# Loading four tiles in place of three by halves on both DMA queues, in a channel-attention kernel

## The chip, the cores and the metric

The kernel runs on one core of a Trainium2 chip. The text names the core's engines as the profile does: PE multiplies matrices, DVE and ACT compute on vectors, and SP only issues transfers here. A transfer is issued into a queue, of SP or of ACT, and 16 DMA engines carry out what both queues hold; a transfer has landed when its last byte has arrived and its waiters may go on.

The metric is the device time of one execution in microseconds (us), lower is better. Most executions of the kernel before took between 531.4 and 532.1 us. A few took more, up to 535.26 us, with no change to the kernel; they are in the comparisons.

A ratio is the mean time of one kernel's fast runs over that of the other's fast runs of the same rounds, so it is not quite the ratio of the medians that I quote. A 95% interval is given with it.

## The reference

```python
def reference(x, w1d):               # x: 1 x 384 x 384 x 384, bf16; w1d: one number
    B, H, W, C = x.shape
    g = jnp.einsum("bhwc->bc", x) / (H * W)      # mean of each channel
    s = _sigmoid(g * w1d[0])                     # (cut: with one tap the padding is none)
    return x * s[:, None, None, :]
```

Every byte of `x` (113.25 MB) must be read and every byte of the result written. In principle a result can only be written when the mean is known, that is after all of `x` has been read, and the kernel's buffer holds only six of the 27 tiles into which it cuts `x`. The kernel therefore makes a guess: it computes the gate `s_early` from the first tile alone and multiplies with it while the true mean is still being summed. At the end it compares the guess with the true gate after rounding. Only if they differ would a second pass run; on this input they are equal.

## The kernel before

A tile is 44 rows of 384 channels on each of 128 partitions: 33,792 bytes a partition, 4.33 MB in all. There are 27 tiles, the last two smaller. The buffer is cut into slots of one tile.

```python
EDGE, SLOT, BOTH = 44, 44, 3
...
n_slots = n_arena // SLOT            # six here
...
def load(place, n, r0, queues=("sync",)):      # SP's queue, if nothing else is said
    of = dram(x_rows, r0, n)
    i = 0
    for queue, m in zip(queues, split(n, -(-n // len(queues)))):
        plan.dma(queue, at(place + i, m), of[:, i * C : (i + m) * C],
                 writes=rows(place + i, m))
        i += m
...
def put(place, n, r0, to):           # DVE multiplies, ACT's queue stores
    plan.op("vector", gate(to, place, n, s_early), ...)
    plan.final.append(
        plan.dma("scalar", dram(o_rows, r0, n), at(to, n), reads=rows(to, n)))
...
for k in range(BOTH):                # the first tiles: half on SP, half on ACT
    load(places[k], sizes[k], starts[k], ("sync", "scalar"))
    if k == 0:
        plan.dma("scalar", w_one[0:1, 0:1], w1d.unsqueeze(0), writes=["w_one"])
...                                  # (cut: s_early from tile 0)
for k in range(1, len(sizes)):
    if k >= n_slots:
        j = k - n_slots
        put(places[j], sizes[j], starts[j], places[j])
    if k >= BOTH:
        load(places[k], sizes[k], starts[k])
    add_rows(places[k], sizes[k], 1, k == 1, k == last)    # PE sums the channels
```

Two queues carry the traffic: SP's and ACT's. Loads wait on SP until the store that used their slot has landed. Stores go through ACT when DVE has multiplied.

## Time and profile before

531.52 us, the median of three runs (531.44 to 531.8).

| what | value | where it is read |
|---|---|---|
| span of the profiled run | 530.0 us | head of the page |
| bytes moved, mean rate | 226.64 MB, 428 GB/s | the page's DMA lines |
| PE, DVE busy | 46%, 46% | part 1 |
| load, from issue to landing | 47.4 us | part 6 |
| store, from issue to landing | 53.6 us | part 6 |

These lines are from the page: busy time by engine; the busy share of the 16 DMA engines in 40 slices (9 is 90% or more); packets; and the two large groups of DMA issues with count, KB of each and us to landing.

```profile
PE 246.4 (46%) x865; PEld 96.0 (18%) x865; DVE 241.3 (46%) x45; ACT 2.7 (1%) x4; POOL 0.3 (0%) x5
DMA  8999999999999999999999999999999999999997
DMA packets 8220, 226.64 MB, mean 428 GB/s; under 512 B 914, under 2 KB 914, under 8 KB 914
...
out_dram<-arena ACTq DMA_DIRECT2D x25, 4224.0 KB, 53.6
arena<-in_x_dram SPq DMA_DIRECT2D x22, 4224.0 KB, 47.4
```

The DMA engines are full from the first slice to the last, and nothing else is. The busy shares of PE and DVE say that they have time to spare. That points to the bytes as what sets the time.

Next, stretches of the run in the view of windows. The first number pair is the stretch in us, the last two columns are the busy share of the DMA engines and their rate in GB/s.

```profile
5.00:30.00 25.00, 14.61 (x60) 6.26 (x61) 5.88 (x9) 0.61 (x1) 0.00 (x0) 1.00 1.01 431
30.00:45.00 15.00, 10.93 (x38) 4.15 (x36) 14.70 (x2) 0.00 (x0) 0.00 (x0) 0.77 1.03 422
45.00:60.00 15.00, 9.69 (x38) 3.79 (x36) 10.88 (x2) 0.00 (x0) 0.00 (x0) 0.89 1.00 433
100.00:480.00 380.00, 179.81 (x627) 69.92 (x627) 171.06 (x20) 0.00 (x0) 0.00 (x0) 0.73 1.00 433
525.00:530.00 5.00, 0.00 (x0) 0.00 (x0) 0.00 (x0) 0.00 (x0) 0.00 (x0) 0.50 0.35 151
```

Loads on both queues (5 to 30 us) run at 431 GB/s, loads and stores together at 433.

Last, the timeline. First three groups of matmuls on PE, which start when their tile lands, with the wait in brackets; then SP's issue of a load in the middle of the run, which waits for a store.

```profile
35.83 10.23 PE L186 MATMUL acc<-arena,ones 128*128 128x512 bf16 x33 [4.07 <-DMA arena<-in_x_dram]
49.34 8.63 PE L186 MATMUL acc<-arena,ones 128*128 128x512 bf16 x33 [3.27 <-DMA arena<-in_x_dram]
...
448.62 8.66 PE L186 MATMUL acc<-arena,ones 128*128 128x512 bf16 x33 [9.85 <-DMA arena<-in_x_dram]
...
61.80 0.33 SPq L91 DMA_DIRECT2D arena<-in_x_dram  x1
401.25 0.33 SPq L91 DMA_DIRECT2D arena<-in_x_dram  x1
```

Tile 2 lands at 35.83 us and tile 3 at 49.34 us. SP issues tile 6 at 61.80 us, when the first store has landed.

### The profile page before, as it was taken

To read this page: it belongs to the slowest core of one execution; us is meant where nothing else is said; L and a number is where in the kernel's file an instruction comes from. 1 tells how busy PE (TensorE), PEld (TensorE's weight loads), DVE (VectorE), ACT (ScalarE), POOL (GpSimd) and SP (SyncE) were. 2 spreads that over 40 slices of the span, in tenths; PEclk is the share of its full clock that TensorE was granted. 3 is DMA by queue.
4 is the path that set the end of the run, shared out by engine and by line. 5 is a ranking of instruction groups with operands and counts; after the bars stand their busy time and mean duration, and the time that the engine had idled before them with its cause. 6 is when DMAs were issued, how large, how long until landed. Compare 5 with 4: busy or idle time off the path is not lost.

```text
span 530.0 us, 1952 instructions
## 1 busy us (share of the span) xinstructions
PE 246.4 (46%) x865; PEld 96.0 (18%) x865; DVE 241.3 (46%) x45; ACT 2.7 (1%) x4; POOL 0.3 (0%) x5
## 2 busy tenths in 40 slices
PE   0867362472472562462572562461562562564320
PEld 0322120120120220120220220120220220221100
DVE  0298715516516426516416426516426426416640
ACT  1000000000000000000000000000000000000000
POOL 0000000000000000000000000000000000000000
PEclk9987876876865776876865766876867766867765
DMA  8999999999999999999999999999999999999997
GB/s 356 431 437 407 441 431 434 436 419 449 434 423 439 426 440 434 423 439 444 421 435 428 441 436 421 441 432 431 436 421 446 435 423 439 423 433 435 439 425 320
DMA packets 8220, 226.64 MB, mean 428 GB/s; under 512 B 914, under 2 KB 914, under 8 KB 914
## 3 DMA queue, kind: packets, MB, share of 16 engines
q10 hardware_dynamic: 4322, 119.74, 52.4%
q1 hardware_dynamic: 3888, 106.76, 47.0%
q8 instruction: 7, 0.11, 0.1%
q14 instruction: 3, 0.02, 0.0%
HBM read 113.25 MB, written 113.25 MB: 427 GB/s over the span
## 4 chain that ended last, share of the span: by engine, by line
another core or an unknown queue 66%; DMA 23%; PE 3%; DVE 2%; SPq 1%; issue 0%; ACTq 0%; ACT 0%; DVEq 0%
DMA arena<-in_x_dram 14%; DMA out_dram<-arena 9%; PE acc L186 3%; DVE arena L156 2%; SPq L91 1%; DVE total L208 0%; ACTq L91 0%; ACT s_true L290 0%; DVE total L298 0%; DVE wrong L306 0%; SPq L99 0%; DVE redo L312 0%; DVEq L99 0%
## 5 line engine op out<-in xcount | busy, mean ns | idle before, releaser
L186 PE MATMUL acc<-arena,ones 128*128 128x512 bf16 x864 | 246.3, 456 | 246.6 <-DMA arena<-in_x_dram 246.6
L156 DVE TENSOR_TENSOR arena<-arena,s_early 128x16896 bf16<-128x16896 bf16 (+2 forms) x27 | 234.6, 8691 | 244.8 <-PE acc L186 241.1
L186 PEld LDWEIGHTS acc<-arena,ones 128*128 128x128 bf16 x864 | 95.9, 114 | 396.5 <-DMA arena<-in_x_dram 254.8
L234 PE MATMUL w_all<-w_one,ones 1*128 1x1 bf16 x1 | 0.2, 158 | 14.4 <-DMA w_one<-in_w1d_dram 14.4
L243 DVE TENSOR_SCALAR w_scaled<-w_all 128x1 f32<-128x1 f32 x2 | 0.2, 153 | 13.6 <-PE w_all L234 13.6
L208 DVE TENSOR_TENSOR total<-total,acc 128x128 f32<-128x128 f32 (+2 forms) x11 | 4.5, 408 | 2.1 <-PE acc L186 1.8
L206 DVE COPY total<-acc 128x384 f32<-128x384 f32 x1 | 0.6, 557 | 8.7 <-PE acc L186 8.7
L290 ACT ACTIVATE s_true<-total,w_scaled 128x384 bf16<-128x384 f32 x1 | 0.6, 615 | 483.3 <-DVE total L208 483.3
L234 PEld LDWEIGHTS w_all<-w_one,ones 1*128 1x128 bf16 x1 | 0.1, 101 | 14.3 <-issue 14.3
L228 ACT ACT_TABLE_LOAD x1 | 1.3, 1283 | 3.0 <-issue 3.0
L298 DVE TENSOR_TENSOR total<-s_true,s_early 128x384 f32<-128x384 uint16 x1 | 0.6, 557 | 0.7 <-ACT s_true L290 0.7
L266 ACT ACTIVATE s_early<-total,w_scaled 128x384 bf16<-128x384 f32 x1 | 0.6, 614 | 21.8 <-DVE total L208 21.8
L306 DVE TENSOR_REDUCE wrong<-total 128x1 f32<-128x384 f32 x1 | 0.6, 552 | 0.0
L256 DVE MEMSET ones<- 128x128 bf16 x1 | 0.2, 165 | 0.8 <-PEq L386 0.8
L228 ACT ACTIVATE warm<-warm 128x1 f32<-128x1 f32 x1 | 0.2, 203 | 0.0
L312 DVE CAST redo<-wrong 128x1 int32<-128x1 f32 x1 | 0.2, 153 | 0.0
L386 POOL MEMSET const-bfloat16-1.0<- 128x1 bf16 x1 | 0.1, 101 | 0.0
L386 POOL MEMSET const-uint8-127<- 128x1 uint8 x1 | 0.1, 101 | 0.0
L255 POOL MEMSET warm<- 128x1 f32 x1 | 0.1, 99 | 0.3 <-POOLq L386 0.3
L386 POOL MEMSET const-float32-0.0<- 128x1 f32 x1 | 0.1, 98 | 0.2 <-issue 0.2
L386 POOL MEMSET const-float32-1.0<- 128x1 f32 x1 | 0.1, 98 | 0.0
## 6 DMA issues: line engine op xcount, KB each, us to landing
out_dram<-arena ACTq DMA_DIRECT2D x25, 4224.0 KB, 53.6
arena<-in_x_dram SPq DMA_DIRECT2D x22, 4224.0 KB, 47.4
arena<-in_x_dram ACTq DMA_DIRECT2D x3, 2112.0 KB, 22.6
arena<-in_x_dram SPq DMA_DIRECT2D x3, 2112.0 KB, 22.3
arena<-in_x_dram SPq DMA_DIRECT2D x1, 2688.0 KB, 43.9
out_dram<-arena ACTq DMA_DIRECT2D x1, 2688.0 KB, 26.5
arena<-in_x_dram SPq DMA_DIRECT2D x1, 2304.0 KB, 39.5
out_dram<-arena ACTq DMA_DIRECT2D x1, 2304.0 KB, 23.9
```

The source lines that it names most:

```text
L91: ("op", lambda e: e.dma_start(out, in_), self.pool[i], 16)
L156: return lambda e: e.tensor_tensor(to_v, v, s_b, ALU.mult)
L186: lambda e, i=i, bank=bank: e.matmul(bank[:, :], ones[:], arena[:, start + i * WIDE : start + (i + 1) * WIDE], start=first and i < 3, stop ...
L206: emit = lambda e, part=part, of=of: e.tensor_copy(part, of)
L208: emit = lambda e, part=part, of=of: e.tensor_tensor(part, part, of, ALU.add)
L228: lambda e: e.activation(warm[:, 1:2], warm[:, 0:1], ACT_F.Sigmoid),
L234: lambda e: e.matmul(w_all[:, 0:1], ones[0:1, :], w_one[0:1, 0:1], start=True, stop=True),
L266: lambda e: e.activation(s_early[:], total[:], ACT_F.Sigmoid, scale=w_scaled[:, 0:1]),
L290: lambda e: e.activation(s_true[:], total[:], ACT_F.Sigmoid, scale=w_scaled[:, 1:2]),
L298: lambda e: e.tensor_tensor(total[:], s_true[:].bitcast(U16), s_early[:].bitcast(U16), ALU.not_equal),
L306: lambda e: e.reduce_max(wrong[:], total[:], axis=mybir.AxisListType.X),
L386: nc = _bacc.Bacc("TRN2", target_bir_lowering=False, num_devices=1)
```

## The change

The intent: tile 3, too, comes in on both queues by rows, half of its rows on each.

```diff
-EDGE, SLOT, BOTH = 44, 44, 3
+EDGE, SLOT, BOTH = 44, 44, 4
```

One load of 128 x 16896 elements on SP becomes two of 128 x 8448, one on SP and one on ACT. Bytes, slots, PE and DVE work stay as they are.

## The prediction

> **What bounds the kernel now.** The transfers, all the way through. The page counts 226.64 MB in a span of 530.0 us, a mean of 428 GB/s, with the DMA engines at nine tenths in 38 of 40 slices; PE and DVE are each busy 46%. In five-microsecond windows the rate is 433 GB/s almost everywhere from 5 to 480 us. The exceptions are the start (230 GB/s in the first 5 us), the place where stores join the loads (409 GB/s from 40 to 45 us), and the end (151 GB/s in the last 5 us). The Trainium skill, "DMA: Bandwidth & Descriptors", section "Where 436 GB/s comes from", gives a ceiling of 435 GB/s for the 16 ports; the trace agrees with its 433. An estimate from the trace: 226.6 MB at 433 GB/s is 523 us, so only about 7 us are start, joins and tail.
>
> **What the change does.** Nothing is removed. By the instruction order one load of 128x16896 on the SP queue becomes two of 128x8448, one on each queue; PE, DVE and POOL are unchanged. The cost is one more issue on the ACT queue, 0.36 to 0.42 us in the trace, at about 3 us, when ACT has only its table load to do. Bytes, the five slots and the waits of later tiles stay.
>
> The same page ("Issuing engines are not separate DMA queues") says that both issuers run on the same 16 engines. The trace agrees: loads on both queues (5 to 30 us) run at 429 to 433 GB/s, loads on one and stores on the other at 433. So a second queue brings no rate; it changes the order of bytes.
>
> **The order.** Before, tile 2 lands at 35.8 us and the first store is issued at 35.86 us. By then about 1.4 MB of tile 3 are in (estimate: 33.4 us at 431 GB/s less three tiles of 4.33 MB). Its rest shares the engines with that store and lands at 49.3 us. After: half of tile 3 stands before the first store on the ACT queue, so I expect tile 3 to land at 43 to 46 us, and the first store at 63 to 66 us instead of 61.8. Tile 5 reuses that store's slot, so its load is issued then, about when tile 4 has ended; the SP queue may stand empty for 1 to 4 us. The stores queued on ACT then take the whole rate, so the engines stay busy (stores alone at the tail still run at 415 to 432 GB/s). After one or two tiles the pattern of before returns: a load issued every 19.95 us, landing about 27 us later.
>
> **On the critical path:** the number of bytes, unchanged. Possible gain: the weak stretch from 30 to 42 us (407 GB/s, about 0.7 us lost) may soften. Possible loss, of the same size: where the SP queue runs dry, and in how unevenly the engines finish (the rate falls from 369 to 18 GB/s between 525 and 529 us).
>
> **Time:** 531.3 us, range 529.8 to 533.2. Chances: faster by over 2% 0.01, within 2% 0.97, slower by over 2% 0.02.
>
> **What would show it.** Right: mean rate still 428 GB/s; windows at 433 after 90 us; PE's wait for tile 3 shorter; the first SP wait for a store slightly longer; the last load at about 500 us. Wrong: windows near 420 GB/s or less every 20 us, with loads landing 20 us after issue rather than 27, which would mean an SP queue that runs dry in every cycle.
>
> **What would make it wrong.** Stores alone being clearly slower than the mix, so that the lost lead matters in every cycle; read and write streams that meet at worse addresses; or a different skew of the engines at the end.

## More of the kernel before

A soft place lies between 30 and 45 us, where the first stores join. There the engines are busy (1.03) and yet move less (422): their packets take longer.

Much later a load is issued at 401.25 us and lands at 448.62 us, 47.4 us after: about two loads stand in SP's queue at any time.

Every experiment was timed beside runs of the kernel before on its own chip.

## The result and the profile after

531.62 us, the median of six runs (531.53 to 532.39), against 531.7 us for the kernel before in six runs (531.44 to 533.69). The ratio is 0.9992, with an interval from 0.9975 to 1.0009: the same time.

The same lines of the page, after:

```profile
PE 246.9 (47%) x865; PEld 96.4 (18%) x865; DVE 241.2 (46%) x45; ACT 2.7 (1%) x4; POOL 0.3 (0%) x5
DMA  8999999999999999999999999999999999999997
DMA packets 8363, 226.62 MB, mean 428 GB/s; under 512 B 930, under 2 KB 930, under 8 KB 930
...
out_dram<-arena ACTq DMA_DIRECT2D x25, 4224.0 KB, 61.5
arena<-in_x_dram SPq DMA_DIRECT2D x21, 4224.0 KB, 39.2
```

The rate is the same. What moved are the two latencies: loads land 8.2 us sooner after their issue, stores 7.9 us later. Their sum is 101.0 us before and 100.7 us after. The stretches, after:

```profile
5.00:30.00 25.00, 15.57 (x59) 6.55 (x60) 4.55 (x9) 0.61 (x1) 0.00 (x0) 1.00 1.00 428
30.00:45.00 15.00, 10.63 (x42) 4.17 (x40) 15.00 (x2) 0.00 (x0) 0.00 (x0) 0.89 1.04 427
45.00:60.00 15.00, 8.97 (x33) 3.55 (x33) 14.25 (x3) 0.00 (x0) 0.00 (x0) 0.82 1.00 431
100.00:480.00 380.00, 179.10 (x627) 69.86 (x627) 171.09 (x20) 0.00 (x0) 0.00 (x0) 0.72 1.00 433
525.00:530.00 5.00, 0.00 (x0) 0.00 (x0) 0.00 (x0) 0.00 (x0) 0.00 (x0) 0.50 0.34 144
```

The soft place is 5 GB/s better before 45 us and 2 GB/s worse after it: it moved with the first store. And the timeline, after:

```profile
46.54 8.97 PE L186 MATMUL acc<-arena,ones 128*128 128x512 bf16 x33 [3.15 <-DMA arena<-in_x_dram]
...
465.54 10.03 PE L186 MATMUL acc<-arena,ones 128*128 128x512 bf16 x33 [10.19 <-DMA arena<-in_x_dram]
...
66.89 0.33 SPq L91 DMA_DIRECT2D arena<-in_x_dram  x1
426.24 0.33 SPq L91 DMA_DIRECT2D arena<-in_x_dram  x1
```

Tile 3 lands at 46.54 us, 2.8 us earlier. The first store has landed at 66.89 us, 5.1 us later. The records of single packets, which the trace holds too, show why: the first packet of the first store moves at 40.7 us before and at 44.4 us after, behind ACT's half of tile 3. The shift of about 8 us is still there late in the run: the load issued at 426.24 us lands 39.3 us later, not 47.4. The last load lands at 497.35 us in place of 500.66, 3.3 us earlier, much as tile 3 did.

### The profile page after: what moved, and what is told of

The parts are those of the page before. It is cut to its first block, busy times and chain, and to the rows that moved or that the text cites. A ratio compares the mean times of both kernels' runs of the same rounds, so it can differ in the third digit from the quotient of the medians.

```text
span 529.9 us, 1954 instructions
## 1 busy us (share of the span) xinstructions
PE 246.9 (47%) x865; PEld 96.4 (18%) x865; DVE 241.2 (46%) x45; ACT 2.7 (1%) x4; POOL 0.3 (0%) x5
## 4 chain that ended last, share of the span: by engine, by line
another core or an unknown queue 70%; DMA 16%; DVE 4%; PE 3%; issue 1%; SPq 1%; ACT 0%; ACTq 0%
DMA out_dram<-arena 8%; DMA arena<-in_x_dram 6%; PE acc L186 3%; DMA w_one<-in_w1d_dram 2%; DVE arena L156 2%; SPq L91 1%; DVE total L208 1%; ACT s_true L290 0%; ACT s_early L266 0%; DVE total L298 0%; DVE total L206 0%; DVE wrong L306 0%; ACTq L91 0%; SPq L99 0%
## 6 DMA issues: line engine op xcount, KB each, us to landing
arena<-in_x_dram SPq DMA_DIRECT2D x21, 4224.0 KB, 39.2
```

## The experiments

Theory A: the time is the number of bytes over one rate of about 433 GB/s, and it does not matter which queue holds them as long as one of the two has work. The rivals are that two queues load faster than one (B), that a gain at the join is cancelled by a loss elsewhere (C), and that a queue that runs dry costs something at each hand-over (D).

### How many tiles are split, and how many slots there are

All loads on SP:

```diff
-    load(places[k], sizes[k], starts[k], ("sync", "scalar"))
+    load(places[k], sizes[k], starts[k])
```

> All loads on the SP queue, none split. Theory A (the time is bytes over one rate of about 433 GB/s, whichever queue carries them): 531 to 533 us. The loads' lead over the stores, which the start sets, shrinks by about 0.7 MB, so loads take about 50 us from issue to landing (47.4 before, 39.2 with four tiles split) in every cycle to the end. Rival B (loads on two queues run faster, and the split start earns its place): slower by 3 us or more, with windows before 30 us clearly under 429 GB/s.

Measured: 532.53 us against 531.63, ratio 1.0004 (0.9985 to 1.0024). Loads took 48.7 us to landing. The window that was to decide:

```profile
5.00:30.00 25.00, 15.91 (x64) 6.75 (x66) 6.72 (x7) 0.62 (x1) 0.00 (x0) 1.00 1.01 438
```

One queue loaded at 438 GB/s, where the split start of the kernel before had 431. The split start earns nothing that can be measured; B falls for the start.

Five tiles split:

```diff
-EDGE, SLOT, BOTH = 44, 44, 3
+EDGE, SLOT, BOTH = 44, 44, 5
```

> Five tiles split. Theory A: 531 to 533 us; another half tile (2.16 MB, 10 us at half of the rate) stands before the first store, so issue to landing falls from 39.2 to about 29 us and stays there; stores rise from 61.5 to about 71 us. Rival C (the equal time of four tiles was a gain at the join that a loss elsewhere cancelled): the time moves by 1 us or more in one direction from three to four to five to six.

Measured: 533.45 us against 531.63, ratio 1.0032 (1.0012 to 1.0051). Loads took 31.0 us, stores 69.8 us. The latencies are near what was expected; the time is about 1.8 us up, which was not (the interval leaves 1 out). The trace shows where it went:

```profile
60.00:100.00 40.00, 13.65 (x49) 5.24 (x48) 22.15 (x3) 0.00 (x0) 0.00 (x0) 0.69 1.00 417
```

By the packet records SP's queue has nothing in flight from 74.4 to 80.7 us. Around its restart, between 70 and 90 us, the packets take 1.3 us longer in sum than at their usual pace (how that is counted is told under "One account").

Six tiles split:

```diff
-EDGE, SLOT, BOTH = 44, 44, 3
+EDGE, SLOT, BOTH = 44, 44, 6
```

> Six tiles split, as many as there are slots, so that all slots are loaded before the first store starts. The SP queue has then nothing to do until the first store has landed, near 77 us, and in each later cycle it holds one load at most: loads about 19 to 20 us from issue to landing. This is the dry queue that my prediction expected of four tiles. Theory A: the stores take the whole rate while SP is dry, time still 531 to 534 us, windows at 433. Rival D (a queue that runs dry costs the hand-over, about 2 us in each of 21 cycles at half of the rate): 540 us or more.

Measured: 533.0 us against 531.63, ratio 1.0021 (1.0001 to 1.0041). Loads took 28.6 us, not 19 to 20, stores 72.3 us. SP issued tile 6 at 75.92 us; tile 5, the last in SP's queue, had landed by 66.18 us. By the packet records SP had nothing in flight from 64.9 to 79.6 us. In that gap the stores ran alone and moved 437 GB/s (66 to 75.9 us). So D, at 540 us or more, falls. The run also corrects me: while SP is dry, the stores go at twice their usual pace, free slots sooner, and SP's queue fills again. The queue ran dry once at length and not in each cycle.

C does not show as it was put: three and four tiles are equal, five and six lie about 1 to 2 us up, six not above five. What five and six lose is not the same thing: five lose it in slow packets at SP's restart, six (whose restart costs 0.3 us) mostly in how unevenly the DMA engines finish, 2.7 us of idle time at the end against 1.9.

Five slots and four tiles split, the case that the prediction really describes (its slots were miscounted, see below):

```diff
-    n_slots = n_arena // SLOT
+    n_slots = 5
-EDGE, SLOT, BOTH = 44, 44, 3
+EDGE, SLOT, BOTH = 44, 44, 4
```

> Four tiles split and five slots in place of six: the kernel that my prediction reckoned with, because it took the slots for five. Theory A: 531 to 534 us; one slot less takes one cycle of 20 us from the loads, so issue to landing is 19 to 20 us in place of 39.2, the same as with six tiles split and six slots. Rival D: 540 us or more, as for six tiles split.

Measured: 532.78 us against 531.63, ratio 1.0016 (0.9998 to 1.0034). Loads took 30.5 us. The first line below is the window from 60 to 100 us, in which SP runs dry and starts again; the second is the rest of the run.

```profile
60.00:100.00 40.00, 16.79 (x53) 6.48 (x55) 13.95 (x2) 0.00 (x0) 0.00 (x0) 0.66 1.01 420
100.00:480.00 380.00, 175.21 (x617) 69.44 (x628) 170.22 (x19) 0.00 (x0) 0.00 (x0) 0.73 1.00 433
```

Here the engines are busy (1.01) and move only 420 GB/s: not idle time, but slower packets. 40 us at 13 GB/s under 433 are 1.2 us. After that the rate is 433 again, so the dry spell was paid once.

Five slots with three tiles split, as a control (the same edit, with `BOTH` left at 3):

> Five slots, three tiles split. Theory A: 531 to 533 us, loads about 27.4 us from issue to landing (47.4 less one cycle of 20), no dry SP queue. With five_slots and four split at 532.8 us this tells what one dry spell costs: I expect 0.5 to 1.3 us, the extra packet time that the trace showed at 70 to 80 us there.

Measured: 531.75 us against 531.72. One of its four runs took 537.52 us, so the ratio, 1.0029 (0.9967 to 1.009), decides little. Loads took 29.0 us, and the window from 60 to 100 us ran at 433. Side by side, the dry spell cost 1.0 us in the medians (532.78 against 531.75, on two chips whose times before were 531.63 and 531.72). The sixth slot by itself buys no time.

### One direction alone

In one kernel the gate and the stores of all tiles but the last were cut, in the other the gate and the loads after the sixth tile; in both the matmuls were cut to six a tile and the second pass was switched off. Their outputs are wrong, which doesn't matter for the times. Each kernel ran once, so its state is unknown; only rates inside one trace are compared. The edits are shown in short; the cuts just named are left out.

```diff
-        if k >= n_slots: put(...)
         if k >= BOTH:
-            load(places[k], sizes[k], starts[k])
+            load(places[k], sizes[k], starts[k],
+                 ("sync",) if k < 15 else ("sync", "scalar"))
```

> Wrong result on purpose: all loads, only the last tile stored, six matmuls a tile in place of 33, no second pass. Tiles 3 to 14 load on SP alone, 15 to 26 by halves on both queues. Theory A: 431 to 434 GB/s in both stretches (40 to 145 us one queue, 165 to 255 us two). Rival B: the stretch with two queues at least 2% faster.

The first two windows are one queue, the last two are both queues:

```profile
40.00:100.00 60.00, 16.05 (x35) 4.39 (x36) 0.00 (x0) 0.00 (x0) 0.00 (x0) 0.63 1.00 432
100.00:145.00 45.00, 8.22 (x18) 2.20 (x18) 0.00 (x0) 0.00 (x0) 0.00 (x0) 0.50 1.00 430
165.00:200.00 35.00, 8.01 (x17) 2.21 (x18) 0.00 (x0) 0.00 (x0) 0.00 (x0) 0.61 1.00 425
200.00:255.00 55.00, 16.45 (x36) 4.40 (x36) 0.00 (x0) 0.00 (x0) 0.00 (x0) 0.62 1.01 427
```

Two queues load no faster than one; here they are about 1% slower, with pieces half as long, so that this run does not say which of the two costs the 1%. B falls.

```diff
-        if k >= BOTH:
+        if BOTH <= k < n_slots:
             load(places[k], sizes[k], starts[k])
+    # in put: no gate; tiles 0 to 11 by halves on ("scalar", "sync"), the rest on ("scalar",)
```

> Wrong result on purpose: six tiles are loaded, then the stores of all 27 tiles run with no loads beside them, tiles 0 to 11 by halves on both queues, the others on ACT alone. Theory A: 431 to 434 GB/s in both stretches (100 to 160 us two queues, 200 to 300 us one). Rival D: stores alone, or one queue alone, 2% or more under 433.

```profile
130.00:160.00 30.00, 0.00 (x0) 0.00 (x0) 0.00 (x0) 0.00 (x0) 0.00 (x0) 0.50 1.01 431
250.00:300.00 50.00, 0.00 (x0) 0.00 (x0) 0.00 (x0) 0.00 (x0) 0.00 (x0) 0.50 1.00 433
```

Stores alone move 431 GB/s from two queues and 433 from one (437 in the window from 200 to 250 us). This is the reason why a queue may run dry unnoticed: the other one, whichever direction it carries, takes the whole rate.

### Why the order of the start is kept to the end

The Trainium skill, "DMA: Bandwidth & Descriptors", section "Queues, rings and completion order", says that an engine goes round the queues that hold work and changes at packets. In this trace the packet records of the loads and stores have 33,792 bytes each, a partition's row of a whole tile (16,896 for half a tile), and the full ones last 1.251 us. If turns go by packet, a piece costs turns and not bytes, and pieces of other sizes must show it.

The kept trace of the kernel before shows the turns themselves. At 101.2 us 13 of the 16 packets in flight are ACT's, at 102.45 us 14 are SP's, at 103.7 us 14 are ACT's again: one packet each, 1.25 us long. The records do not name their DMA engine, but a packet starts 3 to 5 ns before the end of the one that it follows. Between 100 and 480 us, 4092 packets of the two queues can be linked to a packet of one of them in this way, and 4075 times the queue changes.

Tile 3 in four pieces of 11 rows, three on SP and one on ACT:

```diff
-            load(places[k], sizes[k], starts[k])
+            load(places[k], sizes[k], starts[k],
+                 ("sync", "sync", "sync", "scalar") if k == BOTH else ("sync",))
```

> Tile 3 in four pieces of 11 rows, three on SP, one on ACT: half as many bytes (1.08 MB) before the first store as with four tiles split. If the start's order is kept to the end by strict turns of the two queues, issue to landing of loads is about 43 us in every cycle, midway between 47.4 and 39.2; time 531 to 533 us.

```profile
out_dram<-arena ACTq DMA_DIRECT2D x25, 4224.0 KB, 33.5
arena<-in_x_dram SPq DMA_DIRECT2D x21, 4224.0 KB, 69.9
```

I had expected 43 us and the loads went to 69.9 us, the other way. Tile 3 landed at 60.24 us. Turns explain it: on each engine SP needs 3 x 8 = 24 turns for its three quarters (128 partitions over 16 engines are 8 packets a piece), and ACT needs 8 for its own. In the other 16 turns ACT moves full store packets of 33.8 KB. I found this after the result, but the records bear it out: between 42 and 55 us ACT starts 139 full store packets (4.70 MB) and SP 136 quarter packets (1.15 MB). The stores got ahead and stayed there. The time of this run is inconclusive: 536.6 us against 531.72, ratio 1.0070 (1.0007 to 1.0132), but its four runs read 531.93, 536.2, 536.99 and 538.5 us, and I could not settle what the three long ones met.

Tile 3 in two pieces, 33 rows on SP and 11 on ACT:

```diff
+    for queue, m in zip(queues, [33, 11] if r0 == BOTH * SLOT else split(...)):
     # (cut: the load of tile 3 is given both queues)
```

> Tile 3 in two pieces, 33 rows on SP and 11 on ACT: the dose between three and four tiles split, without the small pieces on SP that upset the run with quarters (there loads went up to 69.9 us). If each engine takes one packet from each queue in turn and a packet is one partition's row of a piece, SP's packets are now 25.3 KB and lose a little against the stores' 33.8 KB: issue to landing of loads between 43 and 50 us, constant to the end; time 531 to 533 us in undisturbed runs.

```profile
out_dram<-arena ACTq DMA_DIRECT2D x25, 4224.0 KB, 61.7
arena<-in_x_dram SPq DMA_DIRECT2D x21, 4224.0 KB, 39.2
```

39.2 us, the very number of the half-and-half split, although ACT carried half as many bytes. My expectation of 43 to 50 us was still counting bytes. By turns it had to come out so: both pieces are 8 packets on each engine, whatever their size. The time was 532.19 us against 531.6, ratio 0.9996 (0.9955 to 1.0036).

All loads after the third tile in two pieces of 22 rows, both on SP:

```diff
-            load(places[k], sizes[k], starts[k])
+            load(places[k], sizes[k], starts[k], ("sync", "sync"))
```

> Every load after the third tile in two pieces of 22 rows, both on SP, so that SP's packets are 16.9 KB against 33.8 KB of the stores. Turns by packet: the stores get two thirds while both queues hold work, catch up and wait for the gate; loads rise to 70 to 80 us per tile from issue to landing, stores fall to 20 to 33 us, the last load lands at 515 to 522 us in place of 500.6. Turns by bytes: loads stay at 47 us. The time grows only if the stores left after the last load no longer cover its gate: 531 to 536 us.

```profile
out_dram<-arena ACTq DMA_DIRECT2D x25, 4224.0 KB, 19.9
arena<-in_x_dram SPq DMA_DIRECT2D x47, 2112.0 KB, 79.2
...
100.00:480.00 380.00, 168.50 (x607) 66.41 (x608) 164.65 (x19) 0.00 (x0) 0.00 (x0) 0.73 1.00 423
```

The latencies came out as turns by packet have it: a tile now takes 16 of SP's turns against 8 of ACT's, so stores catch up and wait for DVE. While both queues hold work, from 70 to 99 us, ACT starts 255 packets (8.6 MB) and SP 232 (3.9 MB). The last load lands at 512.2 us, a little before the 515 to 522 us expected. The time did not come out: 543.93 us against 531.6, ratio 1.0234 (1.0185 to 1.0282; at the mark of 2% the record calls that unclear), where I expected at most 536. The window shows where: 423 GB/s with the engines busy (1.00), all through the run. The packets are slower, by 9.2 us in sum from 60 to 480 us. Two causes are possible, the smaller pieces themselves or the stores' queue, which is now without a packet in flight for 94 of these 420 us (11 in the kernel before), 19 times for over 2 us, and starts again each time. The trace speaks for the restarts as the larger part: 5.5 of the 9.2 us fall within the 3 us around each of the 19 restarts (2 us before the first packet to 1 us after it). Where SP's small pieces run alone (36 us in all) the loss is 0.4 us. The other 3.3 us stay unexplained.

### How little slack makes the order matter

Three slots:

```diff
-    n_slots = n_arena // SLOT
+    n_slots = 3
```

> Three slots in place of six. Theory A with a floor: a slot's round is load, gate after PE (about 10 + 9 us), store and two landings, about 42 us when a transfer has the engines alone, against 60 us that three slots allow; SP runs dry often, but the engines have the other queue: 531 to 545 us. Rival D (dry queue costs in each cycle): 560 us or more.

Measured: 560.02 us against 531.6, ratio 1.0517 (1.0468 to 1.0567). Between 100 and 480 us the busy share was 0.98 and the rate 410 GB/s. That is above theory A's range and just inside D's. With three slots each queue is without a packet in flight for 87 us (SP) and 101 us (ACT) of the 420 us from 60 to 480, by the packet records (11 us each in the kernel before), so both run dry again and again; now that does cost.

Two slots and two tiles split:

```diff
-EDGE, SLOT, BOTH = 44, 44, 3
+EDGE, SLOT, BOTH = 44, 44, 2
-    n_slots = n_arena // SLOT
+    n_slots = 2
```

> Two slots, two tiles split. A round of at least 42 us against 40 us that two slots allow at 433 GB/s: now both queues are dry at once at times and the engines stand idle: 570 to 680 us, mean rate 340 to 400 GB/s. Only here should the order of the bytes show in the time.

Measured: 692.31 us against 531.6, ratio 1.3005 (1.2952 to 1.3058), a little over the range. The windows of both runs from 100 to 480 us, three slots first:

```profile
100.00:480.00 380.00, 167.40 (x594) 65.70 (x594) 162.60 (x19) 0.00 (x0) 0.00 (x0) 0.72 0.98 410
```

```profile
100.00:480.00 380.00, 114.67 (x462) 47.16 (x462) 125.06 (x14) 0.00 (x0) 0.00 (x0) 0.66 0.82 342
```

With two slots the engines really stand idle (0.82). With three they do so little (0.98 against 1.00): of the loss between 100 and 480 us about 13 us are slower packets and 7 us idle time.

### One account for the runs

The packet records of the trace allow a sum. A full packet of 33,792 bytes takes 1.251 us at the median. If every byte moved so, the packets would keep each of 16 engines busy for 524.5 us. I add up two things per engine: what the large packets took beyond that pace ("slow packets"), and the time in which fewer than 16 packets were in flight ("idle", from the start of the span to the end of the last packet). Records overlap a little, so only differences against the kernel before are used. The last column is the time of the profiled run less 531.6 us; the profiled run of the kernel before took 531.83 us.

| kernel | slow packets, us | idle, us | sum above before | measured above before |
|---|---|---|---|---|
| before | 2.4 | 4.0 | 0 | 0.2 |
| four tiles split (after) | 2.3 | 4.0 | -0.1 | 0.1 |
| five split | 3.5 | 4.3 | 1.4 | 1.5 |
| six split | 2.4 | 4.9 | 0.9 | 1.0 |
| five slots, four split | 3.6 | 3.6 | 0.8 | 0.9 |
| five slots, three split | 2.1 | 3.8 | -0.5 | 0.0 |
| loads in halves | 11.9 | 4.8 | 10.3 | 10.1 |
| three slots | 18.9 | 17.4 | 29.9 | 29.5 |
| two slots | 18.0 | 149.1 | 160.7 | 160.4 |

The sums agree with the times within about 0.5 us. That is bookkeeping and no test of a cause: the bytes are the same in all rows, so pace, slow packets and idle time must add up to the span. What the table tells is in which of the two terms the time of a run went. The kernels with one queue, with quarters and with 33 and 11 rows are left out, since records of their traces run on past the end of the span.

Before and after are alike in both terms. Of the slow packets, 0.7 us lie between 30 and 40 us before; after, 0.2 us lie there and 0.6 us between 40 and 50 us. In the five-slot run that goes dry, 1.3 us more lie between 70 and 80 us, where the loads start again. So a first meeting or a restart cost between 0.3 us (six tiles split) and 1.3 us in these runs, and the change moves that meeting but does not remove it. Why the packets are slower there was not found.

No run points to a version that beats both kernels. Against the 524.5 us of pure packets, the kernel before has about 2 us of idle at the start, 2 at the end and 2.4 of slow packets, and none of the orders tried here lessens the time by more than the noise.

## Why the prediction was right or wrong

The time was right: 531.3 us predicted, 531.62 measured, in the range of 529.8 to 533.2. What the prediction put on the critical path, "the number of bytes, unchanged", sets it, at a rate that one queue, two queues, loads, stores and their mix all reach within about 3% (425 to 438 GB/s in the windows). It was not luck: with five slots, the case that the prediction had in mind, the time is 532.78 us, still in the range. But its order of events was wrong in the steps told below, which hardly touch the time.

The premise that a second queue brings no rate was right, and the run with loads alone shows it: 430 to 432 GB/s on one queue, 425 to 427 on two. The statement of the Trainium skill, "DMA: Bandwidth & Descriptors", section "Issuing engines are not separate DMA queues", that the transfers of all issuers run on the same 16 engines, agrees.

"The weak stretch from 30 to 42 us", which "may soften", was half right. It softened before 45 us (422 to 427 GB/s) and came back after (433 to 431).

"I expect tile 3 to land at 43 to 46 us, and the first store at 63 to 66 us" had the directions right and both sizes slightly short: 46.54 us, and 66.89 us for the issue that waits for that store. The prediction had the first store share the engines from its issue at 35.86 us on; in the trace before its first packet moves only at 40.7 us, when 3.2 MB of tile 3 are in, not 1.4. PE's wait for tile 3 hardly shrank (3.27 to 3.15 us), since PE was also done with tile 2 earlier, at 43.39 us in place of 46.06.

"The five slots" and "Tile 5 reuses that store's slot" were wrong. There are six. The trace before would have told me in two places: SP issues six loads in the first 4 us, and part 6 gives 47.4 us from issue to landing. I read 27 us, pairing each issue with the tile before its own, and passed over the 47.4. One cycle of 20 us is just the difference.

Hence "the SP queue may stand empty for 1 to 4 us" did not happen after the change: SP held one whole load more than I thought, and from 36 to 480 us its queue is never without a packet in flight for over 0.3 us. With five slots it does happen, and costs about 1 us, once.

"After one or two tiles the pattern of before returns" was the wrong mechanism. With both queues filled, nothing pulls the order back: each engine takes a packet from each queue in turn, so both directions advance alike and the shift of 8.1 us is still there past 400 us. In these runs only a dry queue changed it, as with five and six tiles split, or pieces with shorter rows, as with quarters and halves on SP. I had named "loads landing 20 us after issue" as the sign of a queue that dries in each cycle; the landing times with five slots and four tiles split, 30.5 us, show a queue that does not.

"Stores alone being clearly slower than the mix", my first reason to be wrong, was tested and is false: 431 to 437 GB/s.

## What to carry to other kernels

In this kernel, whose DMA engines are full from start to end, moving bytes from one queue to the other changed who waits and hardly how long it takes (0.3% at most in the runs with six slots and none to six tiles split by halves); only fewer bytes, or less idle and slow time at the ends and joins, would help. Before a prediction rests on a buffer's depth, count the loads that are issued before the first wait, and check the count against the latency from issue to landing divided by the cycle. The two queues shared by packets here, so a piece with shorter rows was not a lighter turn: with one queue's transfers cut in two the other moved twice its bytes while both held work.

## What the Trainium skill lacked or had wrong

- "DMA: Bandwidth & Descriptors", the warning under "Where 436 GB/s comes from": it says that the HBM side (about 358 GB/s) binds transfers between HBM and SBUF. With this one core at work, loads ran at 432, stores at 433 and their mix at 433 GB/s, near the section's 435 GB/s. The condition for the lower figure, that both cores of a pair stream, stands elsewhere on that page, but not in the warning. "HBM Reference", section "Specifications (TRN2)", has both: the share of about 358, and a core alone at about 425 GB/s.
- The same page, "Queues, rings and completion order" and "SWDGE vs HWDGE vs iDMA": a packet is told as some 9 to 17 descriptors, or, for transfers that GpSimd issues, 4096 bytes preferably. Here the records of the SP and ACT queues show packets of 33,792 bytes, a whole row of a partition, and the turns go by them: 33 and 11 rows split like 22 and 22 (39.2 us both), and with halves on SP's queue ACT moved 8.6 MB while SP moved 3.9 (70 to 99 us). Whether these records are the page's packets or its descriptors the trace does not say.
- The same page, "Issuing engines are not separate DMA queues": right on the rate. It lacks that the queue a transfer is put on fixes the lead of loads over stores for the whole run (47.4 or 39.2 us, as long as neither queue runs dry).
- No page that I read has the cost of a direction that starts beside another at full load: 0.3 to 1.3 us of slower packets each time (0.7 us at the join of the kernel before, 1.3 us at the restart with five slots, 0.3 us with six tiles split), with the engines shown as busy.
